# B and C of a chunked scan loaded per batch and turned by VectorE instead of TensorE

## The chip, the cores and the metric

The kernel runs on one core of one Trainium2 chip. The metric is device time of one execution in microseconds (us). Most numbers below are medians of several executions; the profile shows one execution, whose span is one to two us shorter than its time. An execution more than 1.5% above the fastest of its kernel is called slow here and stays out of every ratio. A ratio is the mean time of one kernel's fast runs over the mean of the other's fast runs of the same rounds, on the same chip, so it is not quite the ratio of the medians quoted beside it. The kernel before was timed again with each group of experiments (its medians lie between 132.4 and 133.6 us); the changed kernel was not, so a difference between an experiment's median and the changed kernel's is good to about 1 us only.

## The reference, cut to what matters

Two stages follow each other: a state-space scan over 4 batches x 8 heads x 768 tokens (B and C with 16 columns per token, x with 32), and a gated feed-forward layer over the 3,072 tokens.

```python
# scan, per chunk of tokens: decay, B, C, x -> y and a state that is carried on
cum = np.cumsum(la, axis=-1)                      # la = log(a)
L = np.exp(cum[..., :, None] - cum[..., None, :]) * causal
y_intra = einsum('bhij,bhjd->bhid', einsum('bhin,bhjn->bhij', Cc, Bc) * L, xc)
y_inter = einsum('bhin,bhnd->bhid', Cc, state) * np.exp(cum)[..., None]
state   = decay_full * state + sum_j(B_j x_j * decay_from_j)
# ... then, on tokens x 256 columns
gate = np.maximum(x @ w_gate, 0.0)                # 256 -> 1536
return (gate * (x @ w_val)) @ w_out               # 1536 -> 256
```

The kernels fold the decay into B and C: C is multiplied with the running product of a, B with its inverse. Then chunks of 128 tokens need only products of scaled B and C, a causal mask, and a state matrix.

## The kernel before

Tokens are handled in pairs of chunks: pair p is 256 tokens of all eight heads. Twelve pairs are fed to six feed-forward blocks of 512 tokens. While block b's big matmuls run, the kernel prepares pairs P = 2b+2 and Q = 2b+3: GpSimd scales B and C (`scale`), TensorE turns them (`transp`), VectorE or ScalarE evacuates the turned halves (`tevac`), and TensorE forms the chunk products (`G`, `Dm`, `inter`, `state`).

```python
# B and C of one pair: 64-byte runs (16 columns of a token); the first four pairs 128-byte
q.dma_start(out=bcr[:, i, j], in_=src[b, :, sl, :].rearrange("h s n -> s h n"))
...
def transp(p, k, apart=False):           # both B and C are turned by TensorE
    ...
    for i in range(2):
        nc.tensor.transpose(out=s["tp"][k][:, i], in_=s["tin"][k][i], identity=ident)
...
# in a block: each gv(b, f) is four 512-column matmuls, a Relu on ScalarE, a product on VectorE
for f in range(4, NF):
    gv(b, f)
    if at("scale P", 4, 4, 4):  scale(P, nc.gpsimd, nc.gpsimd)
    if at("turn P", 7, 6, 5):   turn(P); tevac(P, nc.scalar, nc.vector)
    ...
```

In the program a matmul of `gv` needs a free PSUM bank, and a bank becomes free when VectorE has formed the product h from it; that ended one wait of such a matmul before the change (0.2 us). So a VectorE that stands still leaves TensorE only the banks that are free.

## Time and profile before

| | before |
|---|---|
| time, median of four runs at first | 132.38 us |
| TensorE / VectorE / ScalarE / GpSimd busy | 125.6 / 90.1 / 81.7 / 37.6 us of 132.1 |
| granted TensorE clock, mean | 1.00 |
| length of blocks 1 to 4, from first `gv` matmul to first `gv` matmul | 18.9, 18.6, 18.5, 18.4 us |

This profile is of the slowest of its four executions. First the head of the profile page of the kernel before: the span, and each engine's busy time, share and instructions.

```profile
span 132.1 us, 3133 instructions
...
PE 125.6 (95%) x1150; PEld 83.3 (63%) x1157; DVE 90.1 (68%) x196; ACT 81.7 (62%) x177; POOL 37.6 (29%) x76
...
DMA packets 68995, 12.10 MB, mean 92 GB/s; under 512 B 62772, under 2 KB 68980, under 8 KB 68980
```

Then the windows view, one line per stretch (block 0, 1, 2, 3): its bounds and length, then the busy us of TensorE, its weight loads, VectorE, ScalarE and GpSimd, the granted clock, the DMA share and GB/s.

```profile
13.56:37.88 24.32, 23.06 (x228) 15.25 (x226) 17.07 (x36) 15.01 (x36) 8.54 (x15) 1.00 1.11 154
37.88:56.81 18.93, 18.79 (x181) 12.81 (x180) 14.16 (x30) 12.93 (x28) 5.49 (x11) 1.00 0.62 99
56.81:75.43 18.62, 18.57 (x180) 12.69 (x179) 13.47 (x28) 12.93 (x28) 5.55 (x12) 1.00 0.59 85
75.43:93.94 18.51, 18.46 (x180) 12.67 (x180) 13.36 (x27) 12.93 (x28) 5.43 (x11) 1.00 0.60 87
```

TensorE works through the whole of blocks 1 to 3 (18.79 of 18.93 us and so on) at full clock, while VectorE is busy for about 13.5 to 14. So a steady block costs what TensorE's instructions cost, and VectorE has some 5 us to give away per block, but not at every place in it.

The groups view gives the durations that the prediction leaned on (columns: line, engine, operation, output<-inputs, shapes, count | busy us, mean ns of one | idle before it).

```profile
L467 DVE TENSOR_TENSOR h<-r,val 128x512 bf16<-128x512 bf16 x48 | 32.6, 686 | 9.7 <-ACT r L466 8.8 <-PE tp L318 0.7
...
L482 DVE TENSOR_TENSOR h<-r,gv 128x256 bf16<-128x256 bf16 x48 | 19.9, 421 | 7.3 <-ACT r L481 6.9
...
L264 POOL TENSOR_TENSOR bs<-bcr,scaleBC 128x256 bf16<-128x256 f32 x16 | 9.6, 623 | 0.0
...
L352 DVE TENSOR_TENSOR CT<-tp,tmask 128x512 bf16<-128x512 bf16 x8 | 5.5, 686 | 1.6 <-PE tp L318 1.6
```

### The profile page before, as it was taken

The page shows a single profiled execution, that of the slowest core. Times are in us where ns is not written, and L with a number is a line of the kernel's source. Part 1 is how long each engine was busy: PE and PEld are TensorE (multiplying, and loading weights), DVE is VectorE, ACT ScalarE, POOL GpSimd, SP SyncE. Part 2 cuts the span into 40 slices and gives each one's busy share as a digit, 9 for nine tenths or more (in the row PEclk, how much of TensorE's full clock was granted, in tenths as well). Part 3 has the DMA queues.
Part 4 walks back from the last instruction along what each step waited for, and adds up shares of the span by engine and source line. Part 5 has one row for each costly group of instructions (what it writes and reads, how often), then busy time and mean ns, then how long its engine had stood idle before and what let it go on. Part 6 is the DMA issues. An engine that isn't in the chain of part 4 may idle for free.

```text
span 132.1 us, 3133 instructions
## 1 busy us (share of the span) xinstructions
PE 125.6 (95%) x1150; PEld 83.3 (63%) x1157; DVE 90.1 (68%) x196; ACT 81.7 (62%) x177; POOL 37.6 (29%) x76
## 2 busy tenths in 40 slices
PE   6999979999999999999999999999999999999990
PEld 2455655547887457786557785467875577854770
DVE  5648867786478877569977568755879775687511
ACT  4046855393579784488774588744896935876410
POOL 7327374310266000293003390003750022100000
PEclk9999999999999999999999999999999999999999
DMA  3997999996877894239970279761110002200022
GB/s 73 189 183 111 181 210 194 183 144 83 108 136 141 95 118 47 87 86 122 106 83 5 79 137 116 90 64 58 52 57 0 0 0 84 79 0 0 5 88 71
DMA packets 68995, 12.10 MB, mean 92 GB/s; under 512 B 62772, under 2 KB 68980, under 8 KB 68980
## 3 DMA queue, kind: packets, MB, share of 16 engines
q1 hardware_dynamic: 62896, 8.88, 43.7%
q0 software_dynamic: 3184, 2.36, 11.9%
q10 hardware_dynamic: 2896, 0.66, 2.7%
q8 instruction: 9, 0.15, 0.5%
q14 instruction: 10, 0.05, 0.1%
HBM read 11.11 MB, written 3.15 MB: 108 GB/s over the span
## 4 chain that ended last, share of the span: by engine, by line
PE 58%; DVE 1%; issue 0%; DVEq 0%
PE o L490 20%; PE val L463 11%; PE gv L478 11%; PE gate L460 10%; PE y L435 2%; PE g L361 2%; PE A_ps L398 1%; PE tp L318 1%; PE y L424 1%; DVE h L467 0%; DVE ob L503 0%; DVEq L503 0%
## 5 line engine op out<-in xcount | busy, mean ns | idle before, releaser
L467 DVE TENSOR_TENSOR h<-r,val 128x512 bf16<-128x512 bf16 x48 | 32.6, 686 | 9.7 <-ACT r L466 8.8
L490 PE MATMUL o<-wo,h 128*128 128x256 bf16 x288 | 35.0, 273 | 0.1
L466 ACT ACTIVATE r<-gate 128x512 bf16<-128x512 f32 x48 | 28.3, 601 | 8.5 <-PE gate L460 6.2
L369 POOL TENSOR_SCALAR_AFFINE_SELECT gs<-gs 128x512 bf16<-128x512 bf16 (+1 forms) x24 | 12.2, 530 | 65.9 <-ACT gs L380 65.9
L490 PEld LDWEIGHTS <-h 128*128 128x128 bf16 x288 | 27.4, 98 | 5.1 <-issue 1.3
L463 PE MATMUL val<-yT,wv 128*128 128x512 bf16 x96 | 28.6, 379 | 0.3
L460 PE MATMUL gate<-yT,wg 128*128 128x512 bf16 x90 | 27.3, 379 | 0.3 <-ACT r L466 0.3
L482 DVE TENSOR_TENSOR h<-r,gv 128x256 bf16<-128x256 bf16 x48 | 19.9, 421 | 7.3 <-ACT r L481 6.9
L386 DVE TENSOR_TENSOR gs<-g,maskUT 128x512 bf16<-128x512 f32 x24 | 15.5, 686 | 13.0 <-issue 11.8
L481 ACT ACTIVATE r<-gv 128x256 bf16<-128x256 f32 x48 | 18.5, 385 | 2.5 <-PE gv L478 0.9
L478 PE MATMUL gv<-yT,wg 128*128 128x256 bf16 x96 | 18.4, 273 | 0.6 <-ACT yT L448 0.5
L478 PE MATMUL gv<-yT,wv 128*128 128x256 bf16 x96 | 18.3, 273 | 0.0
L463 PEld LDWEIGHTS <-wv 128*128 128x128 bf16 x96 | 9.4, 98 | 11.3
L460 PEld LDWEIGHTS <-wg 128*128 128x128 bf16 x96 | 8.8, 98 | 7.1 <-issue 0.5
L380 ACT CAST gs<-g 128x512 bf16<-128x512 f32 x12 | 7.1, 588 | 9.7 <-PE g L361 9.6
L448 ACT CAST yT<-y 128x512 bf16<-128x512 f32 x12 | 7.0, 586 | 8.2 <-PE y L435 7.1
L478 PEld LDWEIGHTS <-wg 128*128 128x128 bf16 x96 | 9.0, 98 | 2.4 <-issue 1.0
L478 PEld LDWEIGHTS <-wv 128*128 128x128 bf16 x96 | 9.4, 98 | 1.1
L264 POOL TENSOR_TENSOR bs<-bcr,scaleBC 128x256 bf16<-128x256 f32 x16 | 9.6, 623 | 0.0
L506 ACT COPY ob<-o 128x512 f32<-128x512 f32 x10 | 5.9, 586 | 4.7 <-PE o L490 4.7
L163 PE MATMUL w<-warm 128*128 128x512 bf16 x18 | 7.3, 556 | 1.3 <-DVE bcr L81 1.3
L406 DVE TENSOR_TENSOR Sm<-A_ps,smask 128x256 bf16<-128x256 f32 x20 | 8.3, 417 | 0.0
(75 smaller groups left out, 113.1 us busy)
## 6 DMA issues: line engine op xcount, KB each, us to landing
out_dram<-ob SPq DMA_DIRECT2D x10, 256.0 KB, 2.2
xr<-in_x_dram SPq DMA_DIRECT2D x17, 128.0 KB, 3.7
bcr<-in_B_dram SPq DMA_DIRECT2D x16, 64.0 KB, 3.6
bcr<-in_C_dram SPq DMA_DIRECT2D x16, 64.0 KB, 3.3
xr<-in_x_dram SPq DMA_DIRECT2D x3, 256.0 KB, 6.4
wg<-in_moe_w_gate_dram POOLq DMA_DIRECT2D x3, 256.0 KB, 5.0
wv<-in_moe_w_val_dram POOLq DMA_DIRECT2D x3, 256.0 KB, 6.2
wo<-in_moe_w_out_dram POOLq DMA_DIRECT2D x1, 768.0 KB, 11.3
```

What stands on the lines that cost most here:

```text
L264: eng.tensor_tensor(out=bs.rearrange("s k (q t n) -> s k t q n", q=4, t=2)[:, :, t], in0=src[:, :, t], in1=f[:, :, 4 * t:4 * t + 4].to_bro ...
L369: nc.gpsimd.affine_select(out=dst, in_=dst, pattern=[[0, n], [1, 128]], compare_op=ALU.is_ge, fill=0.0, base=0, channel_multiplier=-1)
L386: nc.vector.tensor_tensor(out=d[:, q], in0=g[q], in1=m, op=ALU.mult)
L406: nc.vector.tensor_tensor(out=n, in0=A_ps, in1=smask, op=ALU.mult)
L460: nc.tensor.matmul(out=g, lhsT=wg[:, k, fs], rhs=yT[:, k, tk], start=(k == 0), stop=(k == 1))
L463: nc.tensor.matmul(out=v, lhsT=wv[:, k, fs], rhs=yT[:, k, tk], start=(k == 0), stop=(k == 1))
L466: nc.scalar.activation(r, g, AF.Relu)
L467: nc.vector.tensor_tensor(out=fst[b][:, f], in0=r, in1=v, op=ALU.mult)
L478: nc.tensor.matmul(out=gv_[:, j], lhsT=w[:, k, fs], rhs=yT[:, k, tk], start=(k == 0), stop=(k == 1), skip_group_check=True)
L481: nc.scalar.activation(r, gv_[:, 0], AF.Relu)
L482: nc.vector.tensor_tensor(out=fst[b][:, f, u * 256:(u + 1) * 256], in0=r, in1=gv_[:, 1], op=ALU.mult)
L490: nc.tensor.matmul(out=o[:, ts % 2], lhsT=fst[b][:, f, ts * 128:(ts + 1) * 128], rhs=wo[:, f], start=(f == 0), stop=(f == NF - 1), skip_gr ...
```

## The change

The intent: load B and C of a whole batch at once in long runs, scale them where they land (head-major: a partition holds one row of 24 consecutive tokens, for two heads), and turn 32x32 blocks with VectorE, so that TensorE loses half of its transposes, the token sorts of the first pairs and the decay matmuls. B for the state is still turned back by TensorE. The decay comes from two scans on VectorE. The diff, cut to its core:

```diff
-    NSHARED = 5
+    NSHARED = 6
+    R = 32
+    K = S // R                                   # 24 tokens per row
+    def load_rows(src, b, q, name):
+        rows = glob.tile([128, 2, K * N], FP32, name="%s%d" % (name, b))
+        q.dma_start(out=rows, in_=src[b].rearrange("(t q) (r k) n -> (q r) t (k n)", t=2, r=R))
+        return rows
...
+    def scale_b(b, t, eng):                      # bq: [128, K, 32] bf16
+        eng.tensor_tensor(
+            out=bq[b][:, :, t * N:(t + 1) * N],
+            in0=rows["B", b][:, t].rearrange("p (k n) -> p k n", n=N),
+            in1=FB[:, 2 * b + t].to_broadcast([128, K, N]), op=ALU.mult)
+
+    def turn_b(b, k0=0, k1=K):
+        nc.vector.transpose(BT[b].rearrange("p (r k) -> p k r", k=K)[:, k0:k1], bq[b][:, k0:k1])
+
+    def turn_c(b, t, k0=0, k1=K):
+        nc.vector.transpose(CT[b][:, t].rearrange("p (r k) -> p k r", k=K)[:, k0:k1],
+                            cq[b][:, k0:k1, t])
...
     for b in range(NBLK):
...
-        for n in (P + 2, P + 3):
+        for n in (P + 1, P + 2):
             if n < NPAIR:
-                load(n, nc.sync, nc.sync, nc.sync)
+                load_x(n, nc.sync)
+        if b in (1, 2):
+            for j, src in (("B", B), ("C", C)):
+                rows[j, b + 1] = load_rows(src, b + 1, nc.sync, j.lower() + "r")
...
+            if f in (4, 5):                      # GpSimd: scale B and C of batch b + 1
+                prep(f - 4)
+            if f >= 6:                           # VectorE: one turn of 256 columns per f,
+                prep(f - 4)                      # three more in the out stage
```

Token r*24+k of a head sits in row r. One 32x32 block is one k; after the turn its 32 results belong to tokens k, 24+k, 48+k and so on. In the kernel's order of tokens they are 24 two-byte elements apart: each turn writes with a stride of 48 bytes. Two lines of the diff are side effects: the shared PSUM banks go from 5 to 6, and x of a pair is asked for one pair later than before.

More of the change, by code (lines that the diff above doesn't have):

```diff
@@ L48 @@
     NC = S // 128
-    BH = NB * NH
     DM, DF = moe_w_gate.shape
@@ L55 @@
     NBLK = T // 512
+    R = 32
+    K = S // R
+    MID = 1e27
     const = ctx.enter_context(tc.tile_pool(name="const", bufs=1))
@@ L62 @@
     mm = ctx.enter_context(tc.tile_pool(name="mm", bufs=1, space=bass.MemoryType.PSUM))
-    NSHARED = 5
+    NSHARED = 6
     def bank(name="bank", shape=(128, 512), dtype=FP32):
         return mm.tile(list(shape), dtype, tag="shared", bufs=NSHARED, name=name)
-    NWIDE = 4
     st = {}
-    def wide_bc(p, qb, qc):
-        b, c0 = p // PPB, 2 * (p % PPB)
-        sl = slice(c0 * 128, (c0 + 2) * 128)
-        bcr = raw.tile([128, NH, 2, 2, N], FP32, tag="bcr", name="bcr")
-        for src, j, q in ((C, 1, qc), (B, 0, qb)):
-            if (p, j) in ((0, 0), (2, 1)):
-                nc.vector.memset(bcr[0:1, 0, 0, 0, 0:1], 0.0)
-            q.dma_start(
-                out=bcr[:, :, j].rearrange("p h r n -> p h (r n)"),
-                in_=src[b, :, sl, :].rearrange("h (p r) n -> p h (r n)", r=2))
-        st.setdefault(p, {})["bcr"] = bcr
@@ L87, in wide_x @@
-    def wide_x(p, *qs):
-        b, c0 = p // PPB, 2 * (p % PPB)
-        sl = slice(c0 * 128, (c0 + 2) * 128)
-        xr = raw.tile([128, NH, 2, D], FP32, tag="xr", name="xr")
-        n = NH // len(qs)
-        for k, q in enumerate(qs):
-            hs = slice(k * n, (k + 1) * n)
-            q.dma_start(out=xr[:, hs].rearrange("p h r d -> p h (r d)"),
-                        in_=x[b, hs, sl, :].rearrange("h (p r) d -> p h (r d)", r=2))
-        st.setdefault(p, {})["xr"] = xr
-    def load(p, qx, qb, qc):
-        b, c0 = p // PPB, 2 * (p % PPB)
-        if p < NWIDE:
-            wide_bc(p, qb, qc)
-            wide_x(p, qx)
-        else:
-            xr = raw.tile([128, 2, NH, D], FP32, tag="xr", name="xr")
-            bcr = raw.tile([128, 2, 2, NH, N], FP32, tag="bcr", name="bcr")
-            for i in range(2):
-                sl = slice((c0 + i) * 128, (c0 + i + 1) * 128)
-                qx.dma_start(out=xr[:, i], in_=x[b, :, sl, :].rearrange("h s d -> s h d"))
-                for src, j, q in ((B, 0, qb), (C, 1, qc)):
-                    q.dma_start(out=bcr[:, i, j],
-                                in_=src[b, :, sl, :].rearrange("h s n -> s h n"))
-            st[p] = {"xr": xr, "bcr": bcr}
@@ L115, with load_x @@
-    H = S // 2
-    HC = NC // 2
-    a_sb = glob.tile([2 * BH, H], FP32)
-    nc.sync.dma_start(out=a_sb, in_=a.rearrange("b h (w s) -> (b h w) s", w=2))
+    def load_rows(src, b, q, name):
+        rows = glob.tile([128, 2, K * N], FP32, name="%s%d" % (name, b))
+        q.dma_start(out=rows, in_=src[b].rearrange("(t q) (r k) n -> (q r) t (k n)", t=2, r=R))
+        return rows
+    def load_x(p, *qs):
+        b, c0 = p // PPB, 2 * (p % PPB)
+        xr = raw.tile([128, 2, NH, D], FP32, tag="xr", name="xr")
+        for i in range(2):
+            sl = slice((c0 + i) * 128, (c0 + i + 1) * 128)
+            qs[i % len(qs)].dma_start(out=xr[:, i], in_=x[b, :, sl, :].rearrange("h s d -> s h d"))
+        st[p] = {"xr": xr}
@@ L119 @@
+    al = const.tile([128, 2 * NB, K + 1], FP32)
+    av = a.rearrange("b (t q) (r k) -> (q r) (b t) k", t=2, r=R)
+    nc.sync.dma_start(out=al[:, 0:2, 1:], in_=av[:, 0:2])
+    rows = {}
+    rows["B", 0] = load_rows(B, 0, nc.scalar, "br")
+    rows["C", 0] = load_rows(C, 0, nc.sync, "cr")
+    load_x(0, nc.sync, nc.scalar)
+    nc.sync.dma_start(out=al[:, 2:, 1:], in_=av[:, 2:])
     first = const.tile([1, 2], FP32)
@@ L125 @@
     nc.vector.memset(warm, 0.0)
-    wide_bc(0, nc.scalar, nc.sync)
-    wide_x(0, nc.sync, nc.scalar)
-    wide_bc(1, nc.scalar, nc.sync)
-    wide_x(1, nc.sync)
-    identf = const.tile([2 * BH, 2 * BH], FP32)
-    make_identity(nc, identf)
+    nc.vector.memset(al[:, :, 0:1], 0.0)
+    one = const.tile([128, 2 * NB, K + 1], FP32)
+    nc.vector.memset(one, 0.0)
+    nc.vector.memset(one[:, :, 0:1], 1.0)
+    prod = const.tile([128, R, K + 1], FP32)
+    nc.vector.memset(prod[:, :, K:K + 1], 1.0)
     ident = const.tile([128, 128], BF16)
@@ L135 @@
     make_upper_triangular(nc, maskUT[:, 0], 1.0, diag=True)
-    zero1 = const.tile([2 * BH, 1], FP32)
-    nc.vector.memset(zero1, 0.0)
     tmask = const.tile([128, 2], FP32)
@@ L149 @@
         nc.vector.tensor_scalar_mul(smask[:, t], bd, tmask[:, t:t + 1])
-    pick = const.tile([2 * BH, 2, BH], FP32)
-    pairs = identf.rearrange("p (h w) -> p w h", w=2)
-    nc.vector.tensor_copy(pick[:, 1], pairs[:, 1])
-    order = const.tile([128, 2, 2, 128], BF16)
-    nc.gpsimd.memset(order, 0.0)
-    for r in range(2):
-        nc.gpsimd.tensor_copy(
-            order[:, :, r].rearrange("p c (m r) -> p c m r", r=2)[:, :, :, r],
-            ident.rearrange("p (c m) -> p c m", c=2))
     def keep_warm(n):
@@ L181, in weights_out @@
             in_=moe_w_out[f0 * 128:f1 * 128, :].rearrange("(o i) m -> i o m", i=128))
-    gate = const.tile([1, 4], FP32)
-    def wait_for(p, j):
-        nc.gpsimd.tensor_copy(gate[:, 2 * j:2 * j + 1], st[p]["bcr"][0:1, 0, j, 0, 0:1])
-    wait_for(0, 1)
-    weights(0, 4)
-    cp = glob.tile([2 * BH, H], FP32)
-    nc.vector.tensor_tensor_scan(
-        out=cp, data0=a_sb, data1=zero1.to_broadcast([2 * BH, H]), initial=1.0,
-        op0=ALU.mult, op1=ALU.add)
-    rmid = const.tile([2 * BH, 1], FP32)
@@ L198 @@
-    nc.vector.reciprocal(rmid, cp[:, H - 1:H])
-    nc.vector.tensor_scalar_mul(pick[:, 0], pairs[:, 0], rmid)
-    def wide_decay(ps):
-        d = bank("wdec", (128, len(ps), 2, 8))
-        first = True
-        for k, p in enumerate(ps):
-            b, c0 = p // PPB, 2 * (p % PPB)
-            for i in range(2):
-                w, o = (c0 + i) // HC, ((c0 + i) % HC) * 128
-                for r in range(2):
-                    nc.tensor.matmul(
-                        out=d[64 * i:64 * i + 64, k, r],
-                        lhsT=cp[:, o + r:o + 128:2], rhs=pick[:, w, 8 * b:8 * b + 8],
-                        start=first or (k == 0 and r == 0), stop=True,
-                        tile_position=(0, 64 * i), skip_group_check=True)
-                first = False
-        return d
@@ L218, in wide_factors @@
-    def wide_factors(ps, d):
-        f = const.tile([128, len(ps), 2, 2, 8], FP32, name="wf%d" % ps[0])
-        nc.vector.reciprocal(f[:, :, 0], d)
-        nc.vector.tensor_copy(f[:, :, 1], d)
-        for k, p in enumerate(ps):
-            st[p]["f"] = f[:, k].rearrange("p j r h -> p (j r) h")
-    scaleBC = glob.tile([128, NB, NC, 2, 8], FP32)
-    def decay():
-        d = bank("dec", (128, HC, 2, NB, 8))
-        for k in range(HC):
-            nc.tensor.matmul(
-                out=d[:, k].rearrange("p w b h -> p (w b h)"),
-                lhsT=cp[:, k * 128:(k + 1) * 128],
-                rhs=pick.rearrange("p w h -> p (w h)"),
-                start=(k == 0), stop=True, skip_group_check=True)
-        for w in range(2):
-            cs = slice(w * HC, (w + 1) * HC)
-            nc.vector.reciprocal(
-                scaleBC[:, :, cs, 0, :].rearrange("p b k h -> p k b h"), d[:, :, w])
-        for w in range(2):
-            cs = slice(w * HC, (w + 1) * HC)
-            nc.scalar.copy(
-                out=scaleBC[:, :, cs, 1, :].rearrange("p b k h -> p k b h"), in_=d[:, :, w])
+    gate = const.tile([1, 8], FP32)
@@ new lines, in wait_for, with factors @@
+    def wait_for(j, cell):
+        nc.gpsimd.tensor_copy(gate[:, j:j + 1], cell)
+    FC = const.tile([128, 2 * NB, K], FP32)
+    FB = const.tile([128, 2 * NB, K], FP32)
+    def factors(m0, m1):
+        nc.vector.tensor_tensor_scan(
+            out=prod[:, m0:m1].rearrange("p m k -> p (m k)"),
+            data0=al[:, m0:m1].rearrange("p m k -> p (m k)"),
+            data1=one[:, m0:m1].rearrange("p m k -> p (m k)"),
+            initial=0.0, op0=ALU.mult, op1=ALU.add)
+        tot = const.tile([128, R], FP32, name="tot%d" % m0)
+        nc.vector.transpose(tot, prod[:, :, K])
+        pre = const.tile([128, R], FP32, name="pre%d" % m0)
+        nc.vector.memset(pre[:, 0:1], MID)
+        nc.vector.tensor_tensor_scan(
+            out=pre[:, 1:R], data0=tot[:, 0:R - 1],
+            data1=zero31, initial=MID, op0=ALU.mult, op1=ALU.add)
+        back = const.tile([128, R], FP32, name="back%d" % m0)
+        nc.vector.transpose(back, pre)
+        nc.vector.tensor_tensor(
+            out=FC[:, m0:m1], in0=prod[:, m0:m1, 1:],
+            in1=back[:, m0:m1].to_broadcast([128, m1 - m0, K]), op=ALU.mult)
@@ new lines, in inverse, with clear @@
+    def inverse(b):
+        nc.vector.reciprocal(FB[:, 2 * b:2 * b + 2], FC[:, 2 * b:2 * b + 2])
+    zero31 = const.tile([128, R - 1], FP32)
+    nc.vector.memset(zero31, 0.0)
+    BT = [glob.tile([128, S], BF16, name="BT%d" % b) for b in range(NB)]
+    CT = [glob.tile([128, 2, S], BF16, name="CT%d" % b) for b in range(NB)]
+    bq = [glob.tile([128, K, 2 * N], BF16, name="bq%d" % b) for b in range(NB)]
+    cq = [glob.tile([128, K, 2, 2 * N], BF16, name="cq%d" % b) for b in range(NB)]
+    def clear(b, eng):
+        for t in range(2):
+            eng.memset(cq[b][:, :, t, (1 - t) * N:(2 - t) * N], 0.0)
@@ new lines, in scale_c @@
+    def scale_c(b, t, eng):
+        eng.tensor_tensor(
+            out=cq[b][:, :, t, t * N:(t + 1) * N],
+            in0=rows["C", b][:, t].rearrange("p (k n) -> p k n", n=N),
+            in1=FC[:, 2 * b + t].to_broadcast([128, K, N]), op=ALU.mult)
+    def scale_b(b, t, eng):
+        eng.tensor_tensor(
+            out=bq[b][:, :, t * N:(t + 1) * N],
+            in0=rows["B", b][:, t].rearrange("p (k n) -> p k n", n=N),
+            in1=FB[:, 2 * b + t].to_broadcast([128, K, N]), op=ALU.mult)
@@ L245 @@
+    def turn_b(b, k0=0, k1=K):
[3 more added lines that the diff above has]
+                            cq[b][:, k0:k1, t])
     yT = glob.tile([128, 2, T], BF16)
     A_ps = mm.tile([128, 2, 128], FP32, tag="Aps", name="A_ps")
-    def scale(p, eng, ceng):
-        scale_bc(p, eng)
-        cast_x(p, ceng)
-    def scale_bc(p, eng):
-        b, c0 = p // PPB, 2 * (p % PPB)
-        s = st[p]
-        bs = att.tile([128, 4, 128], BF16, tag="bs", name="bs")
-        if p < NWIDE:
-            src = s["bcr"].rearrange("s (t q) j r n -> s (j r) t q n", t=2)
-            f = s["f"]
-        else:
-            src = s["bcr"].rearrange("s i j (t q) n -> s (i j) t q n", t=2)
-            f = scaleBC[:, b, c0:c0 + 2].rearrange("s c j h -> s (c j) h")
-        for t in range(2):
-            eng.tensor_tensor(
-                out=bs.rearrange("s k (q t n) -> s k t q n", q=4, t=2)[:, :, t],
-                in0=src[:, :, t],
-                in1=f[:, :, 4 * t:4 * t + 4].to_broadcast([128, 4, 4, N]),
-                op=ALU.mult)
-        if p < NWIDE:
-            s["tin"] = [[bs[:, 2 * j + r] for r in range(2)] for j in range(2)]
-        else:
-            s["tin"] = [[bs[:, 2 * i + j] for i in range(2)] for j in range(2)]
-            s["B"] = s["tin"][0]
@@ L275, in cast_x @@
-    def cast_x(p, ceng):
-        s = st[p]
-        cast = ceng.copy if ceng is nc.scalar else ceng.tensor_copy
-        xb = att.tile([128, 2 * NH * D], BF16, tag="xb", name="xb")
-        if p < NWIDE:
-            cast(xb, s["xr"].rearrange("s h r d -> s (h r d)"))
-            s["xw"] = xb.rearrange("s (h r d) -> s r h d", h=NH, r=2)
-        else:
-            cast(xb, s["xr"].rearrange("s i h d -> s (i h d)"))
-            s["x"] = [xb[:, i * NH * D:(i + 1) * NH * D] for i in range(2)]
-    def sort_wide(p, engs=None, own=False):
-        s = st[p]
-        bx = att.tile([128, 2, 384], BF16, tag="bx", name="bx")
-        for i in range(2):
-            if own and i == 0:
-                o = mm.tile([128, 384], FP32, tag="y", name="bxp")
-            else:
-                o = bank("bxp", (128, 384))
-            for r in range(2):
-                nc.tensor.matmul(out=o[:, 0:128], lhsT=order[:, i, r], rhs=s["tin"][0][r],
-                                 start=(r == 0), stop=(r == 1), skip_group_check=True)
-                nc.tensor.matmul(
-                    out=o[:, 128:384].rearrange("s (h d) -> s h d", h=NH),
-                    lhsT=order[:, i, r], rhs=s["xw"][:, r],
-                    start=False, stop=(r == 1), skip_group_check=True)
-            eng = engs[i] if engs else nc.scalar
-            (eng.copy if eng is nc.scalar else eng.tensor_copy)(out=bx[:, i], in_=o)
-        s["B"] = [bx[:, i, 0:128] for i in range(2)]
-        s["x"] = [bx[:, i, 128:384] for i in range(2)]
@@ L307, in transp @@
-    def transp(p, k, apart=False):
-        s = st[p]
-        if "tp" not in s:
-            s["tp"] = {}
-        if apart and k == 0:
-            s["tp"][k] = bank("tpb", (128, 2, 128), BF16)
-        elif not s["tp"]:
-            tp = mm.tile([128, 2, 2, 128], BF16, tag="tp", name="tp")
-            s["tp"] = {0: tp[:, 0], 1: tp[:, 1]}
-        for i in range(2):
-            nc.tensor.transpose(out=s["tp"][k][:, i], in_=s["tin"][k][i], identity=ident)
-    def tevac(p, beng, ceng):
-        s = st[p]
-        tp = s.pop("tp")
-        s["BT"] = BT = att.tile([128, 2, 128], BF16, tag="BT", name="BT")
-        s["CT"] = CT = att.tile([128, 2, 2, 128], BF16, tag="CT", name="CT")
-        wide = p < NWIDE
-        def tokens(k, lead=""):
-            src = tp[k]
-            if wide:
-                return src.rearrange("s r m -> s m r")
-            return src.rearrange("s i m -> s (i m)")
-        def rows(dst):
-            dst = dst.rearrange("s i m -> s (i m)")
-            return dst.rearrange("s (m r) -> s m r", r=2) if wide else dst
-        (beng.copy if beng is nc.scalar else beng.tensor_copy)(rows(BT), tokens(0))
-        if ceng is nc.scalar:
-            for t in range(2):
-                nc.scalar.mul(rows(CT[:, t]), tokens(1), tmask[:, t:t + 1])
-            return
-        src = tokens(1).unsqueeze(1)
-        out_ = CT.rearrange("s t i m -> s t (i m)")
-        if wide:
-            shape = [128, 2, 128, 2]
-            out_ = out_.rearrange("s t (m r) -> s t m r", r=2)
-            mk = tmask.unsqueeze(2).unsqueeze(3)
-        else:
-            shape = [128, 2, 256]
-            mk = tmask.unsqueeze(2)
-        nc.vector.tensor_tensor(out=out_, in0=src.to_broadcast(shape),
-                                in1=mk.to_broadcast(shape), op=ALU.mult)
@@ new lines, in cast_x, with tokens, rows_b @@
+    def cast_x(p, eng):
+        s = st[p]
+        xb = att.tile([128, 2 * NH * D], BF16, tag="xb", name="xb")
+        (eng.copy if eng is nc.scalar else eng.tensor_copy)(
+            xb, s["xr"].rearrange("s i h d -> s (i h d)"))
+        s["x"] = [xb[:, i * NH * D:(i + 1) * NH * D] for i in range(2)]
+    def tokens(p, i):
+        c = 2 * (p % PPB) + i
+        return slice(c * 128, (c + 1) * 128)
+    def rows_b(p):
+        s = st[p]
+        n = 1 if 2 * (p % PPB) + 1 == NC - 1 else 2
+        bb = bank("bb", (128, 2, 128), BF16)
+        for i in range(n):
+            nc.tensor.transpose(out=bb[:, i], in_=BT[p // PPB][:, tokens(p, i)], identity=ident)
+        bt = att.tile([128, 2, 128], BF16, tag="bt", name="bt")
+        nc.scalar.copy(out=bt[:, 0:n], in_=bb[:, 0:n])
+        s["B"] = [bt[:, i] for i in range(n)]
@@ L355, in G @@
     def G(p):
         s = st[p]
+        b = p // PPB
         g = [bank("g%d" % q, (128, 2, 2, 128)) for q in range(4)]
@@ L361, in G @@
                 nc.tensor.matmul(
-                    out=g[q][:, i], lhsT=s["BT"][r, i], rhs=s["CT"][r, :, i],
+                    out=g[q][:, i], lhsT=BT[b][r, tokens(p, i)], rhs=CT[b][r, :, tokens(p, i)],
                     start=(i == 0), stop=True, tile_position=(32 * q, 0),
@@ L424, in inter @@
             nc.tensor.matmul(
-                out=s["y"][:, t, i], lhsT=Sm[:, t], rhs=s["CT"][:, t, i],
+                out=s["y"][:, t, i], lhsT=Sm[:, t], rhs=CT[p // PPB][:, t, tokens(p, i)],
                 start=not s["open"], stop=False, skip_group_check=True)
@@ L508, in foevac @@
             out=out[r0 - 128:r0 + 128, :].rearrange("(i p) m -> p i m", p=128), in_=ob)
-    def turn(p, apart=False):
-        transp(p, 1, apart)
-        transp(p, 0, apart)
-    d0 = wide_decay([0])
-    d1 = wide_decay([1])
-    keep_warm(4)
-    wide_factors([0], d0)
-    scale_bc(0, nc.vector)
-    wide_factors([1], d1)
-    cast_x(0, nc.scalar)
-    turn(0, True)
-    tevac(0, nc.scalar, nc.vector)
-    sort_wide(0, (nc.scalar, nc.vector), own=True)
-    G(0)
-    gevac(0, half=False)
-    state(0, 0)
-    weights(4, 8)
-    load(2, nc.sync, nc.sync, nc.sync)
-    load(3, nc.sync, nc.sync, nc.sync)
-    scale_bc(1, nc.vector)
-    cast_x(1, nc.scalar)
-    keep_warm(7)
+    factors(0, 2)
+    inverse(0)
+    clear(0, nc.gpsimd)
+    wait_for(0, al[0:1, 0, 1:2])
+    weights(0, 4)
+    scale_b(0, 0, nc.vector)
+    scale_c(0, 0, nc.gpsimd)
+    scale_b(0, 1, nc.vector)
+    scale_c(0, 1, nc.vector)
+    load_x(1, nc.sync)
+    turn_b(0)
+    cast_x(0, nc.scalar)
+    keep_warm(10)
+    rows_b(0)
+    turn_c(0, 0)
+    turn_c(0, 1)
+    astep(0, 0)
+    G(0)
+    sevac(0, 0)
+    gevac(0, half=False)
+    wait_for(1, st[1]["xr"][0:1, 1, 0, 0:1])
+    weights(4, 8)
+    load_x(2, nc.sync)
+    rows["B", 1] = load_rows(B, 1, nc.sync, "br")
+    rows["C", 1] = load_rows(C, 1, nc.sync, "cr")
+    keep_warm(4)
     Dm(0)
@@ L537 @@
     yevac(0, nc.scalar)
-    turn(1, True)
-    tevac(1, nc.scalar, nc.vector)
-    sort_wide(1)
+    rows_b(1)
+    cast_x(1, nc.scalar)
     sevac(0, 1)
@@ L548, with prep @@
         more = P < NPAIR
-        for n in (P + 2, P + 3):
+        for n in (P + 1, P + 2):
             if n < NPAIR:
-                load(n, nc.sync, nc.sync, nc.sync)
+                load_x(n, nc.sync)
+        if b in (1, 2):
+            for j, src in (("B", B), ("C", C)):
+                rows[j, b + 1] = load_rows(src, b + 1, nc.sync, j.lower() + "r")
         def at(name, *fs):
             return more and f == fs[min(b, len(fs) - 1)]
+        def prep(step):
+            n = b + 1
+            if n >= NB:
+                return
+            if step < 2:
+                scale_b(n, step, nc.gpsimd)
+                scale_c(n, step, nc.gpsimd)
+            elif step < 5:
+                k = 8 * (step - 2)
+                turn_b(n, k, k + 8)
+            elif step < 11:
+                t, k = divmod(step - 5, 3)
+                turn_c(n, t, 8 * k, 8 * k + 8)
         for f in range(4):
@@ L563 @@
                 weights(8, NF)
-                wait_for(2, 1)
+                wait_for(2, st[2]["xr"][0:1, 1, 0, 0:1])
                 weights_out(0, NF)
+                clear(1, nc.gpsimd)
             if f == (3 if b == 0 else 1):
@@ L578 @@
             if b == 0 and f == 4:
-                wide_factors([2, 3], wide_decay([2, 3]))
+                factors(2, 8)
+                for n in range(1, NB):
+                    inverse(n)
             gv(b, f)
-            if b == 0 and f == 6:
-                decay()
-            if at("scale P", 4, 4, 4):
-                scale(P, nc.gpsimd, nc.gpsimd)
-            if at("scale Q", 8, 5, 4):
-                scale(Q, nc.gpsimd, nc.gpsimd)
-            if at("turn P", 7, 6, 5):
-                turn(P)
-                tevac(P, nc.scalar, nc.vector)
-            if b == 0 and f == 8:
-                sort_wide(P)
+            if f == 4 and b in (1, 2):
+                clear(b + 1, nc.gpsimd)
+            if f in (4, 5):
+                prep(f - 4)
+            if f >= 6:
+                prep(f - 4)
+            if at("cast P", 6, 4, 4):
+                cast_x(P, nc.gpsimd)
+            if at("cast Q", 8, 5, 4):
+                cast_x(Q, nc.gpsimd)
+            if at("rows P", 7, 6, 5):
+                rows_b(P)
             if at("state P0", 9, 8, 7):
@@ L595 @@
                 state(P, 1)
-            if at("turn Q", 99, 9, 8):
-                turn(Q)
-                tevac(Q, nc.scalar, nc.scalar)
+            if at("rows Q", 99, 9, 8):
+                rows_b(Q)
         if more:
@@ L602 @@
         fout(b, 0)
+        prep(8)
         foevac(b, 0)
@@ L606 @@
             gevac(P)
+        prep(9)
+        prep(10)
         if b == 0:
-            turn(Q)
-            tevac(Q, nc.scalar, nc.vector)
+            rows_b(Q)
         fout(b, 1)
         foevac(b, 1)
-        if b == 0:
-            sort_wide(Q)
         if more and b > 0:
```

## The prediction

> # Prediction
>
> **What bounds the kernel.** The page gives TensorE 125.6 us busy of 132.1, VectorE 90.1, ScalarE 81.7, GpSimd 37.6. The windows view of the steady blocks (54.0 to 72.5, 72.5 to 91.0, 91.0 to 109.5 us) shows PE busy 18.45 of 18.50 us and VectorE only 13.35; the chain of waits from 56 us on is TensorE matmuls almost without a gap. Block 0 (13.5 to 37.9 us) is mixed: PE loses about 1.5 us[...].
>
> **What goes.** On TensorE: two of four transposes per pair (0.11 us each pair in the chain, 0.22 per block), the four token sorts (0.7 us each, two in block 0), the decay matmuls in block 0 (0.68 + 0.88 us). On VectorE: the masked CT evacuations (8 x 0.69 us), two 0.73 us reciprocals. On ScalarE about 1 us per block. B and C packets grow from 64 or 128 B to 1,536 B; x stays at 128 B (and for the first four pairs drops from 256 to 128 B).
>
> **What comes.** Three batch turns of 768 columns on VectorE, nine instructions of 256 columns per batch. [...]I estimate 0.42 us each, 3.8 us per batch. The second factor chain costs VectorE about 2.8 us at once in block 0 (scan, two small transposes, product, three reciprocals of 48 elements; estimated from 0.25, 0.35 and 0.73 us for 16, 32 and 96 elements). GpSimd scales 384-element pieces, about 0.9 us each (from 0.62 us for 256).
>
> **By stage.**
> - Prologue: VectorE does three scales (0.56 us each) and three turns (0.95 us) before the first G, against sort and evacuations before: G near 10 us instead of 9.5, gv start within 0.5 us of before.
> - Block 0: PE work falls by about 3 us, but VectorE becomes its limit (about 10.5 us in the gv stage, before 8). Net 0.
> - Blocks 1 and 2: here I expect the loss. The sync queue issues in program order: two x pairs (512 KB of 128 B packets) and then the next batch's B and C (393 KB each), only after the previous block's output, 1.3 us into the block. I estimate B lands 7.3 and C 8.6 us into it. GpSimd then does scale B, scale C, cast of x, scale B in order, until about 11 us. VectorE stands at the first turn (f = 6) from about 8 us; its queue is in order, so h stops, PSUM banks stay full and TensorE stops; the state matmul waits for the x cast as well. About 3 us lost in each of the two blocks.
> - Blocks 3 and 4: PE-bound still, 0.2 us shorter each.
>
> **Time.** 132.6 + 0.2 + 0 + 2 x 3 - 0.5 = about 138 us; range 131 to 142.5. Faster by over 2%: 0.15; within 2%: 0.17; slower by over 2%: 0.68.
>
> **What would show it.** Right: blocks 1 and 2 last 21 to 22 us, blocks 3 and 4 18.3; in the waits VectorE's turn waits for GpSimd's scale, and GpSimd's scale for the row DMAs of batches 2 and 3. The 256-column turns should take 0.40 to 0.45 us. Wrong: no such waits, then blocks 1 to 4 are PE-bound at 18.3 and the time is about 131.
>
> **What would make it wrong.** Rows landing 3 us earlier than estimated[...], VectorE turns with a 48-byte write stride being slower[...], or a prologue delayed by 786 KB of rows competing with the first weights, which no longer wait for C.

132.6 + 0.2 + 0 + 6 - 0.5 comes to 138.3 us. The 0.42 us is an estimate from the trace's products of 256 columns (421 ns, L482 above), and the 0.95 us for 768 columns continues the step from 256 to 512 columns (421 and 686 ns, 1.04 ns per further column). Of DMA the trace shows a share of 1.25 to 1.54 at 183 to 204 GB/s from 18 to 28 us, but also 258 GB/s from 16 to 17 us. B's 7.3 us was estimated; 1.3 us, four issues of x at 0.6 us and 3.6 us from the issue of B to its landing, the last two medians of the trace before, come to the same.

## The result, and the profile after

The changed kernel is right and takes 168.09 us (median of four, 167.0 to 169.4) against 132.38; the ratio of the fast runs is 1.265 (95% interval 1.256 to 1.275). It is far slower than predicted, and outside the range. From here on, lengths of stages are counted from the first VectorE product of one block to that of the next, in the profiled execution:

| us | prologue | block 0 | 1 | 2 | 3 | 4 | rest |
|---|---|---|---|---|---|---|---|
| before | 14.7 | 24.3 | 18.8 | 18.6 | 18.5 | 18.4 | 18.8 |
| after | 23.3 | 30.5 | 28.2 | 30.5 | 18.5 | 18.1 | 18.6 |

So 8.6 us are lost before the first block, 6.2 in block 0, 9.4 and 11.9 in blocks 1 and 2. Blocks 3 and 4, where no batch is prepared any more, are as short as predicted. The page and the same windows, after:

```profile
span 167.7 us, 2899 instructions
...
PE 132.6 (79%) x1062; PEld 82.3 (49%) x1062; DVE 127.3 (76%) x222; ACT 76.0 (45%) x160; POOL 38.6 (23%) x73
...
DMA packets 34685, 12.07 MB, mean 72 GB/s; under 512 B 26480, under 2 KB 34672, under 8 KB 34672
```

```profile
21.84:52.31 30.47, 22.77 (x183) 13.79 (x183) 26.99 (x48) 13.17 (x29) 10.96 (x20) 0.89 0.47 70
52.31:79.95 27.64, 22.08 (x175) 13.96 (x173) 21.25 (x32) 12.24 (x26) 6.18 (x11) 0.84 0.28 68
79.95:111.04 31.09, 22.93 (x177) 13.92 (x175) 25.38 (x40) 12.36 (x26) 8.26 (x15) 0.86 0.24 60
111.04:129.90 18.86, 18.86 (x175) 12.74 (x174) 12.32 (x24) 12.33 (x26) 1.94 (x4) 0.97 0.28 58
```

TensorE now idles for 5.6 us of block 1 and 8.2 us of block 2, and the granted clock of these blocks is 0.84 and 0.86, against 1.00 before. VectorE's busy time is up by 37 us. The groups view says by which instructions:

```profile
L206 DVE STREAM_TRANSPOSE CT<-cq 128x256 bf16<-128x256 bf16 x18 | 22.9, 1403 | 0.0
...
L203 DVE STREAM_TRANSPOSE BT<-bq 128x256 bf16<-128x256 bf16 x9 | 12.0, 1331 | 7.1 <-POOL bq L197 7.1
...
L206 DVE STREAM_TRANSPOSE CT<-cq 128x768 bf16<-128x768 bf16 x2 | 7.4, 3894 | 0.0
...
L203 DVE STREAM_TRANSPOSE BT<-bq 128x768 bf16<-128x768 bf16 x1 | 3.7, 3690 | 0.0
```

A turn of 256 columns takes 1.33 to 1.40 us and one of 768 columns 3.7 to 3.9; the prediction had 0.42 and 0.95. The timeline of VectorE in block 1 (start, duration, instruction, count, and in brackets the idle time before it and what ended it) shows both losses side by side:

```profile
59.57 0.69 DVE L345 TENSOR_TENSOR h<-r,val 128x512 bf16<-128x512 bf16 x1 [0.17 <-ACT r L344]
60.43 0.69 DVE L345 TENSOR_TENSOR h<-r,val 128x512 bf16<-128x512 bf16 x1 [0.17 <-ACT r L344]
64.48 1.35 DVE L203 STREAM_TRANSPOSE BT<-bq 128x256 bf16<-128x256 bf16 x1 [3.35 <-POOL bq L197]
65.45 0.89 DVE L345 TENSOR_TENSOR h<-r,val 128x512 bf16<-128x512 bf16 x1
66.27 1.32 DVE L203 STREAM_TRANSPOSE BT<-bq 128x256 bf16<-128x256 bf16 x1
67.21 0.90 DVE L345 TENSOR_TENSOR h<-r,val 128x512 bf16<-128x512 bf16 x1
```

Up to 60.4 us products come every 0.86 us, at TensorE's pace. Then VectorE waits 3.35 us for GpSimd's scaled B. That is the predicted wait. Afterwards one product and one turn mostly alternate every 1.8 us, twice TensorE's pace for a gv step. That was not predicted. The waits view (who waited for whom, us in total, times, longest) agrees with the first part:

```profile
POOL bq L197 <- DMA br<-in_B_dram: 15.8, 2, 8.6
...
PE A_ps L276 <- DVE Sm L284: 7.3, 3, 3.9
DVE BT L203 <- POOL bq L197: 7.1, 3, 3.5
...
PE A_ps L276 <- POOL xb L215: 4.5, 3, 2.2
```

GpSimd stood 15.8 us in two waits for the rows of B; VectorE stood 7.1 us in three waits for GpSimd. The two lines of `A_ps` say what TensorE itself stood for. `A_ps` is the state matmul. It needs x, which GpSimd casts (`xb`) after its scales of B and C, and a free bank, which VectorE empties (`Sm`). Asked for blocks 1 and 2 alone, the same view gives 1.7 and 2.2 us of waiting for the cast, 3.9 and 3.4 us for `Sm`, which stood behind turns in VectorE's queue, and in block 2 another 1.5 us of the out stage for the last product `h` and 1.0 us for a masked `gs`. That is all of the 5.6 and 8.2 us. No `gv` matmul in these blocks was released by a bank that a product `h` had freed.

### The profile page after: what moved, and what is told of

It reads as the page before. It is cut to its first block, busy times and chain, and to the rows that moved or that the text cites. A ratio compares the mean times of both kernels' runs of the same rounds, so it can differ in the third digit from the quotient of the medians.

```text
span 167.7 us, 2899 instructions
## 1 busy us (share of the span) xinstructions
PE 132.6 (79%) x1062; PEld 82.3 (49%) x1062; DVE 127.3 (76%) x222; ACT 76.0 (45%) x160; POOL 38.6 (23%) x73
## 4 chain that ended last, share of the span: by engine, by line
PE 45%; DVE 27%; POOL 8%; DMA 7%; issue 6%; SPq 3%; ACT 2%; POOLq 0%; DVEq 0%; ACTq 0%
PE o L368 15%; DVE CT L206 13%; PE gate L338 7%; PE gv L356 7%; PE val L341 7%; DVE BT L203 5%; DMA br<-in_B_dram 5%; DVE h L345 4%; SPq L84 3%; POOL bq L197 2%; PE g L240 2%; PE y L313 2%; PE A_ps L276 2%; DMA al<-in_a_dram 1%; PE w L128 1%
## 5 line engine op out<-in xcount | busy, mean ns | idle before, releaser
L368 PE MATMUL o<-wo,h 128*128 128x256 bf16 x288 | 39.2, 294 | 1.5 <-DVE h L345 1.5
L345 DVE TENSOR_TENSOR h<-r,val 128x512 bf16<-128x512 bf16 x48 | 34.8, 728 | 5.4 <-ACT r L344 5.4
L368 PEld LDWEIGHTS <-h 128*128 128x128 bf16 x288 | 29.3, 104 | 10.0 <-issue 3.2
L338 PE MATMUL gate<-yT,wg 128*128 128x512 bf16 x96 | 30.4, 400 | 0.6 <-DVE h L345 0.6
L206 DVE STREAM_TRANSPOSE CT<-cq 128x256 bf16<-128x256 bf16 (+1 forms) x20 | 30.4, 1652 | 0.0
L247 POOL TENSOR_SCALAR_AFFINE_SELECT gs<-gs 128x512 bf16<-128x512 bf16 (+1 forms) x24 | 12.2, 531 | 76.9 <-ACT gs L258 76.9
L203 DVE STREAM_TRANSPOSE BT<-bq 128x256 bf16<-128x256 bf16 (+1 forms) x10 | 15.7, 1567 | 7.1 <-POOL bq L197 7.1
L359 ACT ACTIVATE r<-gv 128x256 bf16<-128x256 f32 x48 | 18.5, 384 | 3.8 <-PE gv L356 1.7
L258 ACT CAST gs<-g 128x512 bf16<-128x512 f32 x12 | 7.0, 587 | 25.4 <-PE g L240 25.3
L341 PEld LDWEIGHTS <-wv 128*128 128x128 bf16 x96 | 9.8, 102 | 12.9 <-issue 2.6
L276 PE MATMUL A_ps<-xb,bt 128*128 128x256 bf16 x20 | 6.2, 310 | 12.2 <-DVE Sm L284 7.3
L284 DVE TENSOR_TENSOR Sm<-A_ps,smask 128x256 bf16<-128x256 f32 x20 | 10.1, 503 | 1.8 <-PE A_ps L276 1.8
L240 PE MATMUL g<-CT,BT 32*128 32x256 bf16 x96 | 5.2, 296 | 7.8 <-DVE CT L206 7.8
```

The source lines that it names most:

```text
L203: nc.vector.transpose(BT[b].rearrange("p (r k) -> p k r", k=K)[:, k0:k1], bq[b][:, k0:k1])
L206: nc.vector.transpose(CT[b][:, t].rearrange("p (r k) -> p k r", k=K)[:, k0:k1], cq[b][:, k0:k1, t])
L247: nc.gpsimd.affine_select(out=dst, in_=dst, pattern=[[0, n], [1, 128]], compare_op=ALU.is_ge, fill=0.0, base=0, channel_multiplier=-1)
L338: nc.tensor.matmul(out=g, lhsT=wg[:, k, fs], rhs=yT[:, k, tk], start=(k == 0), stop=(k == 1))
L341: nc.tensor.matmul(out=v, lhsT=wv[:, k, fs], rhs=yT[:, k, tk], start=(k == 0), stop=(k == 1))
L345: nc.vector.tensor_tensor(out=fst[b][:, f], in0=r, in1=v, op=ALU.mult)
```

## The experiments

Ten kernels were run. They tell apart: (a) a turn that is slow by itself, (b) a destination stride that makes it slow, (c) the late rows, (d) some third cause. The texts number their theories in their own way: Theory 1 there is a stride that slows every instruction, Theory 2 is (a), Theory 3 is a stride that slows the turn alone.

### One cost by itself: `m1_probe`

Behind the changed kernel's last instruction stand groups of three VectorE instructions of 256 elements, with nothing to wait for. It was executed once, like `m2_probe` below, so its state is unknown; only durations of single instructions are read from it.

```diff
+        for _ in range(3):
+            V.transpose(d1, src[:, 0:8])                  # contiguous destination
+        for _ in range(3):
+            V.transpose(d2[:, :, :, 0], src[:, 0:8])      # every 2nd element: 4 bytes
+        ...                                               # 8, 16, 32 bytes
+        for _ in range(3):
+            V.transpose(k8(dk), src[:, 0:8])              # the kernel's own pattern
+        ...                                               # four-byte turns, copies, a product
```

> The changed kernel with VectorE, ScalarE and GpSimd copies added behind its last instruction, three of each, to measure one cost by itself; the time is no verdict. Each probe moves 256 columns of 128 partitions. Theory 1 (a two-byte result written with a stride is slow): turns with a contiguous destination take about 0.42 us, those with the kernel's 48-byte stride about 1.3 us, and a plain copy or product with the same destination stride is slow as well. Theory 2 (the 32x32 turn of two-byte elements is slow by itself, whatever the destination): all bf16 turns take about 1.3 us, four-byte turns 0.42 us, strided copies stay at 0.42 us or less. Theory 3 (only the turn is slow with a strided destination): turns as in theory 1, copies as in theory 2. The probes with strides of 4, 8, 16 and 32 bytes say where the cost begins; the ScalarE and GpSimd probes (768 columns, strided source, contiguous destination) say what a reordering copy would cost there: estimate 0.85 and 0.9 us.

In the groups view L547, L549, L551, L553, L555 are turns of two-byte elements with 2, 4, 8, 16 and 32 bytes between results, L557 has the kernel's pattern; L559 is a contiguous turn of four-byte elements, L563 one in the kernel's pattern (96 bytes); L567 and L571 are a plain copy and a product into the kernel's pattern; L569 is a copy with a strided source and a contiguous destination.

```profile
L557 DVE STREAM_TRANSPOSE dk<-bq 128x256 bf16<-128x256 bf16 x3 | 4.2, 1407 | 0.1
L571 DVE TENSOR_TENSOR tk<-bq 128x256 bf16<-128x256 bf16 x3 | 4.0, 1330 | 0.1
L553 DVE STREAM_TRANSPOSE d<-bq 128x256 bf16<-128x256 bf16 x3 | 3.9, 1312 | 0.1
L555 DVE STREAM_TRANSPOSE d<-bq 128x256 bf16<-128x256 bf16 x3 | 3.9, 1308 | 0.1
L563 DVE STREAM_TRANSPOSE fk<-br 128x256 f32<-128x256 f32 x3 | 2.4, 808 | 0.1
L567 DVE COPY ck<-bq 128x256 bf16<-128x256 bf16 x3 | 2.3, 752 | 0.1
L551 DVE STREAM_TRANSPOSE d<-bq 128x256 bf16<-128x256 bf16 x3 | 2.2, 746 | 0.1
...
L559 DVE STREAM_TRANSPOSE f<-br 128x256 f32<-128x256 f32 x3 | 1.5, 506 | 0.1
L549 DVE STREAM_TRANSPOSE d<-bq 128x256 bf16<-128x256 bf16 x3 | 1.4, 456 | 0.1
L547 DVE STREAM_TRANSPOSE d<-bq 128x256 bf16<-128x256 bf16 x3 | 1.3, 426 | 0.1
L569 DVE COPY cs<-bq 128x256 bf16<-128x256 bf16 x3 | 1.3, 421 | 0.1
```

Theory 2 (slow whatever the destination) falls: the contiguous turn takes 426 ns, what the prediction assumed (and 419 ns inside a kernel, in the next experiment). The time grows with the distance of the two-byte results, up to 1.31 us at 16 bytes, and no more at 32. Theory 3 falls too: the product into the same pattern takes 1,330 ns with no turn in it, and the copy 752 instead of 240. A strided source costs far less (421 ns for the copy). Theory 1 stands: the results' width and distance decide. The reordering copies came to 1.5 us on ScalarE and on GpSimd, not the 0.85 and 0.9 us estimated (in the trace before, other instructions of 256 and 512 columns take 385 and 601 ns on ScalarE and 407 and 635 ns on GpSimd, which continues to 0.82 and 0.86 us for 768); the two ran at the same time, so which of strided source and company costs that is open. VectorE's turns with 2, 4 and 8 bytes ran beside them, all others after them.

That GpSimd's work made the turns slow is excluded by the trace of the changed kernel itself: in the prologue GpSimd executes nothing from 6.6 to 18.9 us, and the three turns there take 3.7 to 3.9 us each.

### The stride taken away: `e1_contig`

```diff
-        nc.vector.transpose(BT[b].rearrange("p (r k) -> p k r", k=K)[:, k0:k1], bq[b][:, k0:k1])
+        nc.vector.transpose(BT[b].rearrange("p (k r) -> p k r", r=R)[:, k0:k1], bq[b][:, k0:k1])
```

The same for C. The tokens are then out of order, so the result is wrong. So that nothing overflows, the decay factors were made harmless (1 for the constant `MID`, a maximum in place of one product; same instruction count).

> Wrong result on purpose: the turns write their destination contiguously (token order inside a batch is then wrong), everything else stays; the factors are made harmless (a maximum in place of the product, the middle value 1) so that nothing overflows. Theory 1 or 3 (destination stride): turns of 256 columns take 0.42 us instead of 1.32, of 768 columns 0.95 instead of 3.69; prologue 8 us shorter, block 0 about 5 us, blocks 1 and 2 about 6 us each; total about 143 us (139 to 147), the waits of VectorE for GpSimd's scale in blocks 1 and 2 stay at 3 to 4 us. Theory 2 (turns slow by themselves): 168 us as before.

142.09 us, ratio to before 1.059 (1.046 to 1.072). The turns now take:

```profile
L206 DVE STREAM_TRANSPOSE CT<-cq 128x256 bf16<-128x256 bf16 x18 | 7.1, 419 | 0.0
...
L203 DVE STREAM_TRANSPOSE BT<-bq 128x768 bf16<-128x768 bf16 x1 | 1.0, 967 | 0.0
```

Prologue 15.3 us (8.0 less), block 0 23.0 (7.5 less), blocks 1 and 2 23.0 and 24.5 (5.2 and 6.0 less). As expected for the stride, and the rival's 168 us did not come. So some 26.0 of the 35.7 us lost are the stride's.

### The rows asked for earlier: `e2_early`

```diff
-        if b in (1, 2):
+        if b in (0, 1):
             for j, src in (("B", B), ("C", C)):
-                rows[j, b + 1] = load_rows(src, b + 1, nc.sync, j.lower() + "r")
+                rows[j, b + 2] = load_rows(src, b + 2, nc.sync, j.lower() + "r")
```

> The rows of batches 2 and 3 are asked for one block earlier, all else as in the changed kernel; the result is right. Theory A (the row loads cost as predicted): VectorE no longer waits 3.35 and 3.50 us for GpSimd's scale in blocks 1 and 2, each block 3 to 6 us shorter (the clock of TensorE also falls less), total 156 to 162 us. Rival (with turns of 1.3 us VectorE is the limit anyway and the wait is hidden): less than 1 us.

159.97 us, ratio 1.198 (1.186 to 1.210), result right: 8.1 us less than the changed kernel, within the range given. Blocks 1 and 2 last 25.0 and 25.4 us; prologue and block 0 are unchanged. VectorE's waits for GpSimd's scaled B have shrunk from 7.1 us to 0.2. So the late rows cost what they seem to cost, also next to slow turns.

### Both: `e3_both`

> Both edits; wrong result on purpose. If slow turns and late rows are the whole loss, blocks 1 and 2 come back to about 18.5 us as blocks 3 and 4, the granted clock to about 1.0, and the total to 132 to 135 us. If a third cause is there (the clock of TensorE, GpSimd, shared PSUM banks), it stays above 138 us.

132.13 us, ratio 0.992 (0.985 to 0.999), wrong result. Blocks 1 and 2 are back at 18.6 and 18.8 us, the clock of its runs at 0.97 to 1.00. The two edits alone give 26.0 and 8.1 us, together 36.0; in ratios, which take out the change of rounds, 0.206 and 0.067, together 0.274. There is no room left for a large third cause that is independent of these two. TensorE's lower clock goes away with them, so it is a consequence. No run separates its own share. The windows allow an estimate: TensorE was busy for 22.08 and 22.93 us in blocks 1 and 2 and for 18.12 us in block 4, at clock 1.00 and with nearly as many matmuls (175, 177 and 174), so about 4 and 5 us of the two blocks' loss came by way of the clock.

### The same turn with four-byte elements: `f1_pair_n`, `f2_pair_j`

A right kernel must keep the order of tokens, and so a stride. But k and k+1 are neighbours in a row and neighbours in the result. If the scales write the two tokens of a pair side by side, the turn can move both as one four-byte element:

```diff
-    bq = [glob.tile([128, K, 2 * N], BF16, name="bq%d" % b) for b in range(NB)]
+    bq = [glob.tile([128, K2, 2 * N, 2], BF16, name="bq%d" % b) for b in range(NB)]   # K2 = K // 2
...
-        nc.vector.transpose(BT[b].rearrange("p (r k) -> p k r", k=K)[:, k0:k1], bq[b][:, k0:k1])
+        nc.vector.transpose(
+            BT[b].bitcast(FP32).rearrange("p (r k) -> p k r", k=K2)[:, k0:k1],
+            bq[b][:, k0:k1].rearrange("p k n j -> p k (n j)").bitcast(FP32))
```

Both kernels also ask for the rows one block earlier. They differ in the inner loop of the scales (16 columns, or the two tokens of a pair).

> A right result: two neighbouring tokens of two bytes each are turned as one four-byte element (the scales write the pairs side by side, their inner loop over the 16 columns), rows one block earlier. Theory 1 or 3 with the probe's numbers[...]: a turn of 256 tokens takes about 0.47 us, of 768 about 1.15 us; total about 132.5 to 134 us, that is within 1.5% of the kernel before. If two-byte width were not the point, turns stay above 0.7 us and the time above 138 us.

> As the other, but the scales' inner loop is over the two tokens of a pair (contiguous writes, source read with a 64-byte stride). If strided two-byte writes cost VectorE and GpSimd in the scales too, this is faster than the other in the prologue by up to 1 us; if short inner loops or strided reads cost more, GpSimd's scales rise above 0.84 us and it is slower.

From the first text a parenthesis is cut that split the probe's time into a fixed part and a part per element; no run shows that split for four-byte turns. As an estimate from what was measured: the changed kernel's turns of 256 and 768 columns (1,331 and 3,690 ns) leave a fixed part of about 0.15 us, and with it the probe's 808 ns give 0.48 and 1.14 us, close to the 0.47 and 1.15 of the text.

Both are right: 130.58 and 130.59 us, ratios 0.984 (0.978 to 0.990) and 0.984 (0.979 to 0.989). They are faster than the kernel before by 1.6%, which leaves the verdict at 2% unclear. The stride is still 48 bytes, but there are half as many elements and each costs less (378 ns for 128 are 2.95 ns each, 1,403 ns for 256 were 5.48):

```profile
L211 DVE STREAM_TRANSPOSE CT<-cq 128x128 f32<-128x128 f32 x18 | 5.9, 378 | 0.0
...
L211 DVE STREAM_TRANSPOSE CT<-cq 128x384 f32<-128x384 f32 x2 | 1.5, 812 | 0.0
...
L205 DVE STREAM_TRANSPOSE BT<-bq 128x384 f32<-128x384 f32 x1 | 0.8, 842 | 0.0
```

The time is 2 us under the lower end of the estimate; one reason is that the turns take 0.38 to 0.39 and 0.81 to 0.85 us, not 0.47 and 1.15. The estimate had used the probe with 96 bytes between results (808 ns), the kernel has 48. That this is the whole of the 2 us was not tested. The inner loop makes no difference to the time; GpSimd's scales take 0.84 to 0.88 us in the first and 0.88 to 0.90 in the second.

### Late rows with fast turns: `f0_pair_late`

Pair turns, but the rows as late as in the changed kernel: the change as the prediction imagined it.

> Right result: pair turns alone, the rows of batches 2 and 3 asked for as late as in the changed kernel. This prices the late rows with turns as fast as the prediction assumed. By the difference of the two contiguous kernels (142.1 and 132.1 us) it should be 8 to 10 us slower than the pair kernel with early rows (130.6): 138 to 141 us, near the predicted 138; blocks 1 and 2 last 21 to 24 us. If pair turns leave VectorE enough slack to hide the wait: under 133 us.

139.37 us, ratio 1.048 (1.041 to 1.056). The prediction was 138. Blocks 1 and 2 last 22.4 and 24.2 us, where 21 to 22 had been predicted. Its waits view:

```profile
POOL bq L192 <- DMA br<-in_B_dram: 14.6, 2, 7.5
DVE BT L205 <- POOL bq L192: 9.6, 3, 5.4
...
PE A_ps L282 <- POOL xb L221: 7.0, 3, 4.1
```

The last line is the one that costs time. In blocks 1 and 2 TensorE's only waits in this view are 2.3 and 4.1 us of the state matmul for GpSimd's cast of x. So with fast turns the late rows reach TensorE through GpSimd, which stands at the scale of B with the cast behind it. That path was in the prediction ("the state matmul waits for the x cast as well"); its other path, VectorE's products and full banks, ended no wait here.

### More strides: `m2_probe`

> The pair kernel with more probes of VectorE behind its end, 256 elements of 128 partitions each, contiguous source; the time is no verdict. If what costs is a two-byte result at any wide stride, the bf16 turns lie between the earlier ones (6-byte stride between 0.46 and 0.75 us, 12-byte between 0.75 and 1.3), four-byte turns stay at 0.4 to 0.6 us for all strides up to 48 bytes, and a bf16 copy and a bf16 product at a 32-byte stride are slow as well (0.75 and 1.3 us), with no turn in them. If the wide product of the first probe was slow for its two sources and not for its destination, the bf16 product at a 32-byte stride takes 0.4 us. The four-byte copy and product at a 48-byte stride: 0.4 us if width decides, over 0.7 if stride alone does.

All times of the two probe runs for 256 elements, in ns, by the distance in bytes of neighbouring results (those of 48 and 96 bytes marked k have the kernel's pattern, in which the 32-result blocks interleave):

| | 2 | 4 | 6 | 8 | 12 | 16 | 32 | 48 | 48 k | 96 k |
|---|---|---|---|---|---|---|---|---|---|---|
| turn, two-byte | 426 | 456 | 586 | 746 | 1016 | 1312 | 1308 | | 1407 | |
| turn, four-byte | | 473 to 506 | | 432 | | 613 | 622 | 611 | | 808 |
| copy, two-byte | 240 | 303 | | 449 | | 747 | 776 | | 752 | |
| copy, four-byte | | | | | | 459 | | 390 | | |
| product, two-byte | | 443 | | | | | 1227 | | 1330 | |
| product, four-byte | | | | | | | | 672 | | |

The lines of this run for the turn at 12 bytes (L543), the product at 32 bytes (L567) and the four-byte product at 48 bytes (L569):

```profile
L567 DVE TENSOR_TENSOR q<-s 128x256 bf16<-128x256 bf16 x3 | 3.7, 1227 | 0.1
L543 DVE STREAM_TRANSPOSE q<-s 128x256 bf16<-128x256 bf16 x3 | 3.0, 1016 | 0.1
...
L569 DVE TENSOR_TENSOR q<-s 128x256 f32<-128x256 f32 x3 | 2.0, 672 | 0.1
```

The two-byte copy and product at 32 bytes are slow without any turn (776 and 1,227 ns, against 303 and 443 at 4 bytes). Four-byte results also pay for a wide stride, but less: 613 against 1,312 ns for a turn at 16 bytes, 459 against 747 for a copy. The four-byte copy at 48 bytes (390 ns) came out as expected if width decides; the four-byte product, at 672 ns, lies between the two outcomes. For two-byte results the pattern is a cost that rises with the distance up to 16 bytes and then stays (1,312 and 1,308 ns, 747 and 776). Up to there the copy's times (240, 303, 449, 747 ns at 2, 4, 8 and 16 bytes) rise by about 36 ns per byte of distance, and the turn's by about 73 ns per byte from 6 bytes on (586 to 1,312 ns), both estimates from the table. In the kernels, from 256 to 768 columns, a turn of B costs 4.6 ns per further column with the 48-byte stride (1,331 and 3,690 ns) and 1.04 ns without it (433 and 967 ns in `e1_contig`). What makes the strided two-byte result dear was not settled: the runs show the cost by distance and width, and no run separates causes.

### Rows in the out stage: `f3_rows_mid`, `f4_wo_free`

In the pair kernel the first out matmul waited 1.3 us for the last weights, which were loading together with the early rows. These two ask for the rows of the batch after next behind the first output of the block; the second also drops GpSimd's gate in front of those weights.

```diff
         fout(b, 1)
         foevac(b, 1)
+        if b in (0, 1):
+            for j, src in (("B", B), ("C", C)):
+                rows[j, b + 2] = load_rows(src, b + 2, nc.sync, j.lower() + "r")
```

> Right result: pair turns, rows of the next batch but one asked for in the out stage of the block before (after its first output) instead of at the block's start, so that they do not compete with the last weights in block 0. In the pair kernel the first out matmul waits 1.3 us for those weights. If that wait goes: 129.3 to 130.2 us. If the rows come too late again in block 1: over 131 us.

> As rows_mid, and GpSimd no longer holds the last weights back until x of pair 2 has landed. If the weights still bound the first out stage: another 0.3 to 1 us less; if x of pair 2 or 3 then lands too late, equal or slower.

Both are right: 129.28 and 129.12 us, ratios 0.973 (0.968 to 0.978) and 0.973 (0.968 to 0.977). They beat the kernel before (132.63 us in those rounds). Dropping the gate adds nothing that the intervals could tell. Blocks 0, 1 and 2 of the former last 22.2, 18.2 and 18.3 us. This is what the change was meant to give: 2 us in block 0, 0.3 to 0.5 us in blocks 1 to 4, and now nothing paid for it (the prologue is 14.1 us, before 14.7).

## Why the prediction was wrong

- **The step that failed** is this one: "I estimate 0.42 us each, 3.8 us per batch." The 0.42 us measured in the trace belong to products that wrote contiguously. With results of two bytes 48 bytes apart a turn of 256 columns took 1.33 to 1.40 us. By the two contiguous kernels this step is worth 26.0 us with late rows and 27.8 us with early ones (`e2_early` less `e3_both`). The prediction named the 48-byte stride among the things that could make it wrong, but its range of 131 to 142.5 us had no room for it.
- **Prologue** ("gv start within 0.5 us of before"): wrong by 8 us through the same term, three turns of 3.7 to 3.9 us in a row. With the stride gone it was 15.3 us against 14.7, and 13.2 with late rows and pair turns.
- **Block 0** ("Net 0"): 6.2 us longer; with contiguous turns 1.3 us shorter than before.
- **Blocks 1 and 2** ("About 3 us lost in each"): the chain from rows to scale to turn was right, the size too small. Of the two ways in which it was to stop TensorE, the traces show the wait for the cast of x; full banks behind a standing `h` ended no wait of TensorE there. Counted from block 1's first matmul (52.3 us), GpSimd had the rows of B at 61.3 us, 9.0 us into it, not 7.3; VectorE's first turn began 12.2 us into it, not at 11. With fast turns the two blocks came to 22.4 and 24.2 us, 3.6 and 5.6 us above before. Asking for the rows earlier took away 8.1 us with slow turns and 10.0 with contiguous ones.
- **Blocks 3 and 4** ("0.2 us shorter each"): 18.46 and 18.12 against 18.51 and 18.40 us, in sum right.
- **The sum**: the error is 30.1 us. With the turns at the assumed cost (`e1_contig`: 0.42 and 0.97 us) the time was 142.1 us against the predicted 138, so the turn makes some 26 of it; most of the rest are the late rows, which cost 10.0 us in blocks 1 and 2 instead of 6. `f0_pair_late` came nearer to 138, with 139.4, by luck: its late rows cost 9.2 us, 3 more than predicted, while its prologue and block 0 were 1.5 and 2.1 us shorter than before, where the prediction had +0.2 and 0.
- **Not foreseen**: TensorE's clock. In the windows view of the changed kernel the granted clock is 0.50 from 92 to 98 us, after TensorE had been busy for 1.78 of the 4 us before, so it had not been idle throughout. It is 0.83 from 98 to 100 us and 1.00 in the window after that; TensorE was busy for all of the two windows from 96 to 100.

```profile
88.00:90.00 2.00, 0.86 (x4) 0.29 (x3) 0.69 (x1) 0.79 (x2) 1.20 (x2) 1.00 0.19 65
90.00:92.00 2.00, 0.92 (x5) 0.52 (x5) 0.00 (x0) 0.18 (x1) 2.00 (x4) 0.96 0.00 0
92.00:94.00 2.00, 2.00 (x8) 0.82 (x6) 1.58 (x2) 1.23 (x3) 1.19 (x2) 0.50 0.00 0
94.00:96.00 2.00, 0.53 (x2) 0.10 (x1) 2.00 (x4) 0.15 (x1) 0.00 (x0) 0.50 0.00 0
96.00:98.00 2.00, 2.00 (x6) 0.73 (x5) 2.00 (x3) 0.60 (x1) 0.00 (x0) 0.50 0.00 0
98.00:100.00 2.00, 2.00 (x14) 1.25 (x13) 2.00 (x4) 0.60 (x1) 0.00 (x0) 0.83 0.00 0
100.00:102.00 2.00, 0.58 (x5) 0.22 (x3) 2.00 (x4) 0.00 (x0) 0.00 (x0) 1.00 0.00 0
```
